# Loads gated on the fifth exponentials, products without use at the start, and a longer load latency in the planner of a Linformer attention and MLP-mixer kernel

## The chip, the cores and the metric

The kernel runs on one core of one Trainium2 chip, in one launch. The metric is the device time of one execution in microseconds (us), as the median of the runs. A separate execution was taken by the hardware profiler; all rows, windows and transfers quoted here come from that one.

## The reference

For 8 batches, 8 heads, 1024 positions and 64 channels in a head, attention with projected keys and values (`E` and `F` are 64 x 1024), then an MLP mixer over positions (256 wide) and over channels (512 to 1536 to 512):

```python
k_proj = einsum('ks,bhsd->bhkd', E, k);  v_proj = einsum('ks,bhsd->bhkd', F, v)
scores = q @ k_proj.T / 8;  attn = softmax(scores)         # over 64 projected keys
x = (attn @ v_proj).transpose(0, 2, 1, 3).reshape(B, S, H * D)
h = relu(x.transpose(0, 2, 1) @ w_tok1) @ w_tok2
u = x + h.transpose(0, 2, 1)
out = u + relu(u @ w_ch1) @ w_ch2
```

Inputs and output are float32; the kernel works in bf16 with float32 sums.

## The kernel before

**Two parts for each batch.** `front(b)` does attention and the token mixer, `channel(b)` the channel mixer. In a front, a projection multiplies k and v with E and F (L423 and L427, side by side in the two halves of TensorE's columns; batch 0 uses L484 and L491). `attend(h)` scores each head (L535), VectorE takes the maxima and subtracts them (L544, L545), ScalarE takes the exponentials (L551), and the weights are transposed, from batch 1 on by a DMA transpose that SP issues (L578, tile `eT`; batch 0 uses TensorE, L586, with a copy, L589). In batch 0, for the heads in `DIRECT`, the subtraction is folded into eight small ScalarE instructions (L564, with L557 and L558 on VectorE). `weigh` multiplies the weights with v for a group of heads (L630) and normalises (L596, L597, L642); the groups are heads 0 to 2, 3 to 5, and 6 and 7 from batch 1 on. `tok1` (L662) and `tok2` (L750; batch 0 L692) are the token mixer; their sum `u` is transposed for the channel mixer (`uT`: by SP from batch 1 on, L769; batch 0 by TensorE, L733). q is transposed by TensorE in batches 0 and 1 (L518) and by SP from batch 2 on (L794). `channel(b)` multiplies up (L860, 96 matmuls of 512 columns in a batch) and down (L903), adds `u` (L914) and stores (L919, SP).

**The order of instructions is planned.** Each step is an operation with an engine (or a choice of two), an estimated time, dependences, buffers and a rank. `Planner.plan` walks through estimated time: of the operations that are ready it takes the one that could start first, the front's before the channel's where both could, and writes it at the end of its engine's queue. On the chip each engine keeps to that order and waits by semaphores where the estimate was too short. Loads are issued by POOL, and the planner keeps one clock for all transfers:

```python
dma = max(t + w + 1.8, dma) + o.dma                      # a load from POOL, w = 0.72
dma = max(t + 1.0, dma) + o.dma                          # a transfer from SP; end = dma + 1.0 + DMA_SLACK
```

`o.dma` is the transfer's size by an assumed rate (`READ`, `WRITE`, `TURN`), and `DMA_SLACK` is 1.5 us.

**When loads are issued.** All of batch 0, the first weights and batch 1 are issued from the start, in the order of `LOADS`: a small letter with a number is a pair of heads of batch 0, a capital one a half of batch 1, `wt1`, `wt2` and `wc1a`, `wc1b` are weights. Everything later waits behind a gate: `later(at, *seen)` looks `at` up in `GATES`, and where there is an entry, POOL copies one element of a tile (L331, `mark`), so that it waits until that tile is written, and then issues the loads of the entry (L290; the halves of `w_ch2`, `w0` and `w1`, L337). The key `(b, h)` waits for the `eT` of head h of batch b, `(b, "t")` for the last `uT` of batch b - 1 and the last q transpose of batch b, `(b, "u")` for the last `uT` of batch b. Batches share five input buffers (`ins_pool`), each of which holds the k, the v or the q of one batch.

`RK` holds the ranks of batch 0's projections, weighings and token mixing.

Of the kernel before, what the change touches and what calls it, by code (L numbers as in the profile page):

```python
# [16 lines left out]

LOADS = ("k0", "q0", "q1", "k1", "k3", "v1", "q3", "k2", "q2", "v0", "wt1", "v3", "wt2", "v2",  # L20
         "V0", "wc1a", "K0", "Q0", "Q1", "V1", "K1", "wc1b")
GROUPS0 = ((0, 1), (2, 3), (4, 5), (6, 7))
DIRECT = (5, 7)
ADDED = (0, 1, 2, 3)
SUMMED = (0, 1, 2, 3)
RK = (-37, -7, 82)


GATES = {(0, "u"): ("w0",), (1, 0): ("w1",), (1, 4): ("k2", "v2", "q2"), (1, "u"): ("k3",), (2, "t"): ("v3",),
         (2, 7): ("q3",), (3, "t"): ("k4", "v4"), (3, 7): ("q4",), (4, "t"): ("k5", "v5"),  # L30
         (4, 7): ("q5",), (5, "t"): ("k6", "v6"), (5, 7): ("q6",), (6, "t"): ("k7", "v7"), (6, 7): ("q7",)}


AFTER = {"PE": 0.2, "DVE": 0.15, "ACT": 0.15}
# [4 lines left out]
def dve(n, kind="f32"):  # L39
    return 0.08 + (0.00104 * n + 0.075 if kind == "f32" else 0.00052 * n + 0.07)  # L40
# [35 lines left out]
class Planner:  # L76
# [6 lines left out]
    def op(self, eng, fn, deps=(), new=(), bufs=(), prio=0, dma=0.0, behind=()):  # L83

        o = Op()
        o.eng, o.fn, o.deps, o.new = eng, fn, [d for d in deps if d], list(new)
        o.prio, o.dma = prio, dma
        o.bufs = list(dict.fromkeys(list(new) + list(bufs)))
        for b in o.bufs:
            b.left += 1  # L90
        o.seq, o.waiting, o.after, o.ready = len(self.ops), 0, [], 0.0
        o.behind, o.next = list(behind), []
        self.ops.append(o)
        return o

    def plan(self, start):
        for o in self.ops:
            o.waiting = len(o.deps) + len(o.behind)
            for d in o.behind:
                d.next.append(o)  # L100
            for d in o.deps:
                d.after.append(o)
        free = dict(start)
        dma = 3.4
        ready = [o for o in self.ops if not o.waiting]
        order = []
        while ready:
            best = None
            for o in ready:
                at = o.ready  # L110
                ok = all(b.slot is not None or b in o.new for b in o.bufs)
                for b in o.new:
                    slot = b.pool.best()
                    ok = ok and slot is not None
                    at = max(at, slot[0]) if slot else at
                if not ok:
                    continue
                for e, w in o.eng.items():
                    key = (max(at, free[e]), o.prio, w, o.seq)
                    if best is None or key < best[0]:  # L120
                        best = (key, o, e)
            assert best is not None, "no operation can go on"
            (t, _, w, _), o, e = best
            ready.remove(o)
            for b in o.new:
                f, i = b.pool.best()
                b.pool.free_at[i] = None
                b.slot = i
            if e == "POOL":
                free[e] = t + w  # L130
                if o.dma:
                    dma = max(t + w + 1.8, dma) + o.dma
                    end = dma + (DMA_SLACK if o.prio[0] > 0 else 0.0)
                else:
                    end = t + w + 0.3
            elif e == "PE":
                free[e] = t + w
                end = t + w + AFTER[e] + (SLACK if o.prio[0] > 0 else 0.0)
            elif e == "SP":
                free[e] = t + w  # L140
                dma = max(t + 1.0, dma) + o.dma
                end = dma + (1.0 if o.prio[0] >= 0 else 0.6) + (DMA_SLACK if o.prio[0] % 2 == 0 else 0.0)
            else:
                free[e] = t + w - 0.08
                end = t + w + AFTER[e] - 0.08 + (SLACK if o.prio[0] > 0 else 0.0)
            for b in o.bufs:
                b.left -= 1
                b.until = max(b.until, end)
                if not b.left:
                    b.pool.free_at[b.slot] = b.until  # L150
            for a in o.after + o.next:
                a.waiting -= 1
                a.ready = max(a.ready, end if a in o.after else t)
                if not a.waiting:
                    ready.append(a)
            order.append((t, end, e, o))
        assert len(order) == len(self.ops)
        return order
# [3 lines left out]
def kernel(  # L162
# [13 lines left out]
    nc = tc.nc  # L176
    P = 128

    B, H, S, D = q.shape
# [26 lines left out]
    bank_any = Pool_(banks)  # L206
# [17 lines left out]
    ident = sb.tile([P, P], BF16, name="ident")  # L224
# [20 lines left out]
    op = pl.op  # L245

    def f32(buf, *shape):
        t = buf.t
        n = 1
        for s_ in shape:  # L250
            n *= s_
        t = t[:, :n]
        if len(shape) == 2:
            return t.rearrange("p (a b) -> p a b", b=shape[1])
        return t
# [19 lines left out]
    def load(fn, prio, nbytes, deps=(), new=(), bufs=()):  # L275
        behind = [latest[0]] if latest else []
        latest[:] = [op({"POOL": 0.72}, lambda e: fn(), deps, new, bufs, prio, nbytes / READ, behind)]
        return latest[0]
# [35 lines left out]
    ld = {}  # L314
    for name in LOADS:
        if name in weights:
# [8 lines left out]
    def later(at, *seen):  # L325

        what = GATES.get(at)
        if not what:
            return
        b = at[0]  # L330
        gate = [op({"POOL": 0.1}, lambda e, of=of: nc.gpsimd.tensor_copy(out=mark, in_=of()), [dep], [],  # L331
                   [buf], prio=(2 * b, 0, len(pl.ops))) for buf, of, dep in seen]
        for w in what:
            if w[0] == "w":
                cs = slice(int(w[1]) * CC // 2, (int(w[1]) + 1) * CC // 2)
                ld_wc2[int(w[1])] = load(
                    lambda cs=cs: nc.gpsimd.dma_start(  # L337
                        out=wc2_sb[:, cs, :], in_=moe_w_ch2.rearrange("(cc p) d -> p cc d", p=P)[:, cs, :]),
                    (0, len(pl.ops)), DM * DC * 2, gate)
            else:  # L340
                load_in(int(w[1]), w[0], 0, H, (2 * b, 0, len(pl.ops)), gate)

    mk_ident = op({"POOL": 0.55}, lambda e: make_identity(nc, ident), prio=(0, 0.5))


    stage = Buf(gT_pool)
# [6 lines left out]
    for i, w in enumerate((E, F)):  # L353
# [3 lines left out]
        for g in range(2):  # L357
# [14 lines left out]
            def ef_c(e, i=i, sl=sl, pb=pb):  # L372
                if i == 0:
                    copier(e)(out=EFT_sb[:, sl, :KP], in_=b16(pb, NSI, KP)[:, sl])
                else:
# [4 lines left out]
            o = op({"ACT": 1.15, "DVE": 0.7}, ef_b, [ld_ef], [], [stage], (0, -90 + i, g))  # L380
            o = op({"PE": 0.5}, ef_t, [o, mk_ident], [pb] if g == 0 else [], [pb, stage],
                   prio=(0, -90 + i, g))
# [6 lines left out]
    def last_u(b):  # L389
        return uTs[b], lambda: uTs[b].t[0:1, NSI - 1, 0, 0:1], uT_at[b][NSI - 1][-1]  # L390
# [4 lines left out]
    def front(b):  # L395
# [8 lines left out]
        def pr():  # L404
            n_[0] += 1
            return (lvl, rank[0], n_[0])
# [6 lines left out]
        qTb = Buf(qT_pool)  # L413
# [97 lines left out]
        def attend(h):  # L511
# [56 lines left out]

            if first and h in DIRECT:
                om = op({"DVE": dve(512) + 0.2}, rmax, [os_], [], [sc, mx], pr())  # L570
# [221 lines left out]
        if b >= TURN_Q:  # L792
            for h0 in range(0, H, 4):
                o = op({"SP": 3.5}, lambda e, h0=h0: nc.sync.dma_start_transpose(  # L794
                    out=qTb.t[:, h0 : h0 + 4].rearrange("p h t c -> p (h t) c"),
                    in_=qin.t[:, h0 : h0 + 4].rearrange("p h s d -> p (h s d)")),
                    [landed[b, "q", h0]], [qTb] if h0 == 0 else [], [qin, qTb], pr(),
                    dma=4 * S * D * 2 / TURN)
                for h in range(h0, h0 + 4):
                    qt_at[h] = o  # L800
            later((b, "t"), last_u(b - 1), (qTb, lambda: qTb.t[0:1, H - 1, 0, 0:1], o))
        for h0, h1 in chunks:
            rank[0] = RK[0] + 2 * h0 if first else 0
            (project_first if first else project)(h0, h1)
            for h in range(h0, h1):
# [5 lines left out]
                if h in group_of_last:  # L811
                    rank[0] = 2 * h + RK[1] if first else 0
                    if first and group_of_last[h] in SUMMED:
# [3 lines left out]
                    if first:  # L817
                        heads = groups[group_of_last[h]]
                        rank[0] = 2 * h + RK[2]
                        for i in range(TC):  # L820
# [14 lines left out]
    def channel(b):  # L835
# [92 lines left out]
        for si in range(NSI):  # L928
            if (b, si) == (B - 1, NSI - 1):
                down_by_columns(si, (DM // 2, DM // 4, DM // 4))  # L930
            else:
                down(si)

    front(0)
    for b in range(B):
        if b + 1 < B:
            front(b + 1)
        channel(b)
# [35 lines left out]
```

## Time and profile before

| | |
|---|---|
| median of 3 runs (lowest, highest) | 471.61 us (470.45, 471.82) |
| the profiled execution's own time | 473.21 us |
| its span | 471.3 us |
| TensorE busy | 454.7 us (96%) |
| VectorE, ScalarE busy | 271.2 us (58%), 177.6 us (38%) |
| mean granted TensorE clock | 0.993 |
| read from HBM, written to it | 59.24 MB, 16.78 MB |

The span runs from the first instruction to the last; 1.9 us of the profiled execution's time lie around it. A row of the timeline gives the start, the length, the engine, the line, the operation with what it writes and reads, and how many instructions are merged; in brackets stands the idle time of the engine before it and what ended that. Where a row merges several matmuls, its end holds the last one's way through the array, so a matmul's cost is taken from the distance of starts: 0.216 us for 512 columns at the full clock.

### The profile page before, as it was taken

To read this page: it belongs to the slowest core of one execution; us is meant where nothing else is said; L and a number is where in the kernel's file an instruction comes from. 1 tells how busy PE (TensorE), PEld (TensorE's weight loads), DVE (VectorE), ACT (ScalarE), POOL (GpSimd) and SP (SyncE) were. 2 spreads that over 40 slices of the span, in tenths; PEclk is the share of its full clock that TensorE was granted. 3 is DMA by queue.
4 is the path that set the end of the run, shared out by engine and by line. 5 is a ranking of instruction groups with operands and counts; after the bars stand their busy time and mean duration, and the time that the engine had idled before them with its cause. 6 is when DMAs were issued, how large, how long until landed. Compare 5 with 4: busy or idle time off the path is not lost.

```text
span 471.3 us, 7555 instructions
## 1 busy us (share of the span) xinstructions
PE 454.7 (96%) x2916; PEld 238.4 (51%) x2916; DVE 271.2 (58%) x624; ACT 177.6 (38%) x333; POOL 37.3 (8%) x67
## 2 busy tenths in 40 slices
PE   4799996999999999999999999999999999999996
PEld 3696553445545445545554455545545455544444
DVE  5987673349475579439655478528665388521022
ACT  4867630117510472207610374116520375105600
POOL 7420020010000100010000100010000000000000
PEclk9999998899999999999999999999999999999999
DMA  9999999889689896879489995889489221351022
GB/s 168 208 207 208 166 152 236 149 165 171 98 175 179 171 171 113 185 143 226 70 164 184 197 160 77 175 176 226 74 163 194 90 56 35 57 167 45 1 89 91
DMA packets 122885, 68.14 MB, mean 145 GB/s; under 512 B 86752, under 2 KB 114272, under 8 KB 122848
## 3 DMA queue, kind: packets, MB, share of 16 engines
q0 software_dynamic: 28192, 29.36, 39.9%
q1 hardware_dynamic: 94656, 38.29, 38.2%
q8 instruction: 23, 0.38, 0.3%
q14 instruction: 14, 0.11, 0.1%
HBM read 59.24 MB, written 16.78 MB: 161 GB/s over the span
## 4 chain that ended last, share of the span: by engine, by line
PE 89%; DMA 6%; ACT 2%; POOL 1%; DVE 1%; issue 0%; POOLq 0%
PE bank L860 34%; PE bank L903 33%; PE bank L662 6%; PE bank L750 5%; DMA in<-in_v_dram 3%; PE bank L535 3%; PE bank L630 3%; PE bank L423 2%; DMA in<-in_q_dram 1%; DMA eT<-ex 1%; PE bank L692 1%; PE bank L427 1%; ACT ex L551 1%; PE bank L518 1%; PE bank L733 0%
## 5 line engine op out<-in xcount | busy, mean ns | idle before, releaser
L860 PE MATMUL bank<-uT,wc_sb 128*128 128x512 bf16 x768 | 178.6, 379 | 0.0
L903 PE MATMUL bank<-wc_sb,gT 128*128 128x512 bf16 x756 | 171.4, 379 | 0.0
L265 ACT ACTIVATE gT<-bank 128x512 bf16<-128x512 f32 x169 | 100.5, 595 | 96.9 <-PE bank L860 95.4
L903 PEld LDWEIGHTS <-gT 128*128 128x128 bf16 x756 | 72.5, 98 | 82.8 <-issue 1.6
L860 PEld LDWEIGHTS <-wc_sb 128*128 128x128 bf16 x768 | 71.7, 98 | 73.8 <-issue 0.2
L914 DVE TENSOR_TENSOR o<-bank,u 128x512 f32<-128x512 f32 x63 | 43.3, 690 | 109.4 <-PE bank L903 109.3
L544 DVE TENSOR_REDUCE mx<-bank 128x8 f32<-128x512 f32 x62 | 42.3, 682 | 30.1 <-PE bank L535 30.1
L642 DVE TENSOR_TENSOR x<-bank,rd 128x384 bf16<-128x384 f32 (+1 forms) x100 | 48.7, 498 | 3.5 <-ACT ex L564 0.5
L545 DVE TENSOR_TENSOR sh<-bank,mx 128x512 f32<-128x512 f32 x62 | 42.9, 692 | 4.6
L759 DVE TENSOR_TENSOR u<-bank,x 128x512 bf16<-128x512 f32 x56 | 34.2, 683 | 18.0 <-PE bank L750 18.0
L551 ACT ACTIVATE ex<-sh 128x512 bf16<-128x512 f32 x62 | 39.0, 629 | 9.2 <-DVE sh L545 7.3
L437 ACT CAST kp<-bank 64x512 bf16<-64x512 f32 (+1 forms) x8 | 4.2, 525 | 85.1 <-PE bank L427 84.9
L662 PE MATMUL bank<-x,wt_sb 128*128 128x512 bf16 (+1 forms) x176 | 30.4, 328 | 0.0
L630 PEld LDWEIGHTS <-eT 128*128 128x128 bf16 x256 | 19.0, 97 | 13.3 <-issue 1.2
L750 PE MATMUL bank<-hT,wt_sb 128*128 128x512 bf16 x112 | 25.3, 379 | 0.0
L630 PE MATMUL bank<-vbd,eT 128*128 128x130 bf16 x256 | 23.9, 220 | 1.1 <-DVE sh L545 0.7
L535 PEld LDWEIGHTS <-qT 128*128 128x128 bf16 x256 | 18.3, 100 | 9.7 <-ACT qT L528 0.2
L265 ACT ACTIVATE hT<-bank 128x512 bf16<-128x512 f32 (+1 forms) x20 | 9.2, 473 | 35.8 <-PE bank L662 35.6
L535 PE MATMUL bank<-kbd,qT 128*128 128x128 bf16 x256 | 22.3, 222 | 0.2 <-ACT qT L528 0.2
L662 PEld LDWEIGHTS <-wt_sb 128*128 128x128 bf16 x176 | 14.7, 99 | 14.8 <-issue 2.6
L750 PEld LDWEIGHTS <-wt_sb 128*128 128x128 bf16 x112 | 16.1, 144 | 8.4
L427 PE MATMUL bank<-in,EFT_sb 128*64 128x512 bf16 (+1 forms) x64 | 15.3, 386 | 3.8 <-DMA in<-in_v_dram 3.8
(72 smaller groups left out, 228.0 us busy)
## 6 DMA issues: line engine op xcount, KB each, us to landing
out_dram<-o SPq DMA_DIRECT2D x63, 256.0 KB, 2.6
in<-in_k_dram POOLq DMA_DIRECT2D x6, 1024.0 KB, 10.3
in<-in_v_dram POOLq DMA_DIRECT2D x6, 1024.0 KB, 16.8
in<-in_q_dram POOLq DMA_DIRECT2D x6, 1024.0 KB, 9.8
wc_sb<-in_moe_w_ch_dram POOLq DMA_DIRECT2D x4, 768.0 KB, 20.7
in<-in_k_dram POOLq DMA_DIRECT2D x4, 256.0 KB, 7.3
in<-in_q_dram POOLq DMA_DIRECT2D x4, 256.0 KB, 7.6
in<-in_v_dram POOLq DMA_DIRECT2D x4, 256.0 KB, 11.1
```

What stands on the lines that cost most here:

```text
L265: nc.scalar.activation(out=out, in_=in_, func=ACT.Relu)
L535: nc.tensor.matmul(f32(sc, NT, 2 * KP)[:, t, :], qT.t[:, h, t, :], bd.t[0][:, h // 2, h % 2, :], start=True, stop=True,)
L544: nc.vector.reduce_max(out=mx.t, in_=s_, axis=AX.X)
L545: nc.vector.tensor_tensor(out=sh.t, in0=s_, in1=mx.t[:, :, None].to_broadcast([P, NSI, KP]), op=ALU.subtract,)
L551: nc.scalar.activation(out=ex.t, in_=sh.t.rearrange("p (t s) k -> p t (s k)", s=2), func=ACT.Exp, scale=scale,)
L630: nc.tensor.matmul(ou[:, i], eTs[h].t[:, t, :], bd.t[1][:, h, :], start=True, stop=True)
L642: nc.vector.tensor_tensor(out=xb.t[:, t, heads[0] : heads[0] + n], in0=ou[:, :, :, 0:D], in1=r.to_broadcast([P, n, 2, D]), op=ALU.mult,)
L662: nc.tensor.matmul(f32(pb, n), wt1_sb[:, si, i * P : (i + 1) * P], xrow(si, a, z), start=(si == 0), stop=(si == NSI - 1),)
L750: nc.tensor.matmul(f32(pb, DM), wt2_sb[:, i, si::NSI], hb.t[:, i, :], start=(i == 0), stop=(i == TC - 1),)
L860: nc.tensor.matmul(f32(pb, 4, P), wc1_sb[:, dc, cc * P : (cc + 1) * P], uT.t[:, sj * 4 : (sj + 1) * 4, dc, :], start=(dc == 0), stop=(dc = ...
L903: nc.tensor.matmul(f32(pb, DM), g.t[:, cc, (si % 4) * P : (si % 4 + 1) * P], wc2_sb[:, cc, :], start=(cc == 0), stop=(cc == CC - 1),)
L914: nc.vector.tensor_tensor(out=ob.t, in0=f32(pb, DM), in1=u.t[:, si, :], op=ALU.add)
```

## The change

- `LOADS` has another order: q1 ahead of q0, q3 ahead of k3, `wt2` ahead of v3, and K0 ahead of V0, K1 ahead of V1, Q1 last, with `wc1a` ahead of them all.
- `DIRECT` holds heads 2, 3, 4, 5 and 7 of batch 0 instead of 5 and 7.
- `FILL` adds 40 matmuls of the identity with itself at the start, of the lowest rank, whose result nobody reads.
- `RK` has other values.
- `GATES`: in batches 1 to 6 the k, v and q of the next batch are issued together when the `eT` of head 4, the fifth, has landed. For batch 1 this is so before. For the others, before, k and v waited for `(b, "t")` (k3 for `(1, "u")`), and q for the `eT` of head 7. The call with `(b, "t")` is gone.
- The planner takes a load's latency as 3.8 us instead of 1.8.

Line numbers in the text are those of the kernel before.

```diff
--- before.py
+++ after.py
@@ -17,18 +17,18 @@
 
 
 
-LOADS = ("k0", "q0", "q1", "k1", "k3", "v1", "q3", "k2", "q2", "v0", "wt1", "v3", "wt2", "v2",
-         "V0", "wc1a", "K0", "Q0", "Q1", "V1", "K1", "wc1b")
+LOADS = ("k0", "q1", "q0", "k1", "q3", "k3", "v1", "k2", "q2", "v0", "wt1", "wt2", "v3", "v2",
+         "wc1a", "K0", "V0", "Q0", "K1", "V1", "Q1", "wc1b")
 GROUPS0 = ((0, 1), (2, 3), (4, 5), (6, 7))
-DIRECT = (5, 7)
+DIRECT = (2, 3, 4, 5, 7)
 ADDED = (0, 1, 2, 3)
 SUMMED = (0, 1, 2, 3)
-RK = (-37, -7, 82)
-
-
-GATES = {(0, "u"): ("w0",), (1, 0): ("w1",), (1, 4): ("k2", "v2", "q2"), (1, "u"): ("k3",), (2, "t"): ("v3",),
-         (2, 7): ("q3",), (3, "t"): ("k4", "v4"), (3, 7): ("q4",), (4, "t"): ("k5", "v5"),
-         (4, 7): ("q5",), (5, "t"): ("k6", "v6"), (5, 7): ("q6",), (6, "t"): ("k7", "v7"), (6, 7): ("q7",)}
+FILL = 40
+RK = (-16, -9, 96)
+
+
+GATES = {(0, "u"): ("w0",), (1, 0): ("w1",),
+         **{(b, 4): (f"k{b + 1}", f"v{b + 1}", f"q{b + 1}") for b in range(1, 7)}}
 
 
 AFTER = {"PE": 0.2, "DVE": 0.15, "ACT": 0.15}
@@ -129,7 +129,7 @@
             if e == "POOL":
                 free[e] = t + w
                 if o.dma:
-                    dma = max(t + w + 1.8, dma) + o.dma
+                    dma = max(t + w + 3.8, dma) + o.dma
                     end = dma + (DMA_SLACK if o.prio[0] > 0 else 0.0)
                 else:
                     end = t + w + 0.3
@@ -343,6 +343,13 @@
     mk_ident = op({"POOL": 0.55}, lambda e: make_identity(nc, ident), prio=(0, 0.5))
 
 
+    idle = Buf(bank_any)
+    for i in range(FILL):
+        op({"PE": 0.09}, lambda e: nc.tensor.matmul(
+            f32(idle, P), ident, ident, start=True, stop=True), [mk_ident],
+            [idle] if i == 0 else [], [idle], (99, i))
+
+
     stage = Buf(gT_pool)
     eft = {}
 
@@ -798,7 +805,6 @@
                     dma=4 * S * D * 2 / TURN)
                 for h in range(h0, h0 + 4):
                     qt_at[h] = o
-            later((b, "t"), last_u(b - 1), (qTb, lambda: qTb.t[0:1, H - 1, 0, 0:1], o))
         for h0, h1 in chunks:
             rank[0] = RK[0] + 2 * h0 if first else 0
             (project_first if first else project)(h0, h1)
```

## The prediction

> **What bounds the kernel now.** I read first the busy rows and slices of the page, then TensorE's waits and timeline, then the loads.
>
> ```profile
> PE 454.7 (96%) x2916; PEld 238.4 (51%) x2916; DVE 271.2 (58%) x624; ACT 177.6 (38%) x333; POOL 37.3 (8%) x67
> PE   4799996999999999999999999999999999999996
> PEclk9999998899999999999999999999999999999999
> ```
>
> TensorE is the bound: full in all slices but the first three, the seventh and the last. So only two places can give time, the first 25 us and the neighbourhood of 80 us; a new wait of TensorE anywhere else adds its whole length. The seventh and eighth slices also show the granted clock dip. Here is TensorE's timeline there (start, us, what):
>
> ```profile
> 76.34 0.40 PE L423 MATMUL bank<-in,EFT_sb 128*64 128x512 bf16 x1
> 80.53 0.59 PE L427 MATMUL bank<-in,EFT_sb 128*64 128x512 bf16 x1 [3.79 <-DMA in<-in_v_dram]
> ...
> 84.04 4.67 PE L662 MATMUL bank<-x,wt_sb 128*128 128x512 bf16 x16
> 88.54 1.89 PE L903 MATMUL bank<-wc_sb,gT 128*128 128x512 bf16 x8
> ```
>
> And the windows around it (TensorE's busy time is the third number, the granted clock stands behind the engines):
>
> ```profile
> 80.00:84.00 4.00, 3.47 (x15) 1.48 (x14) 0.00 (x0) 0.00 (x0) 0.00 (x0) 0.50 1.18 252
> 84.00:90.00 6.00, 6.00 (x24) 2.50 (x24) 0.69 (x1) 2.35 (x4) 0.00 (x0) 0.82 0.60 109
> ```
>
> The projection of batch 2 waits 3.79 us for its v, and then the clock is at 0.50. From 76.34 to 88.54, 12.2 us, TensorE did a projection and `tok1`. At the full clock these take 8 pairs at 0.216 (1.7 us) and 3.56 (the chain's L662 row of the next batch): 5.3 us. The wait therefore cost 6.9 us, 3.8 idle and 3.1 of slow work.
>
> **The gates, batch 1 to 2: a gain of 6.7 us.** Gate (1,4) is the same in both. What differs is TensorE's order: I summed the changed program's matmuls in their order at 0.2158 (512 columns), 0.058 (130) and 0.056 (128) us. Between the first projection of batch 1 and that of batch 2 lie 42.05 us of work instead of 38.6, since `tok1` (16 matmuls, 3.45) now stands ahead. TensorE comes to the projection at 76.34 + 3.45 = 79.8 instead of 76.3; v landed at 80.5. It also scores head 4 some 2.4 us earlier, so the gate opens no later. A rest of 0 to 0.7 us stays, too short to resemble the one idle time after which the clock fell; I take 0.2. Gain 6.9 - 0.2 = 6.7.
>
> **The gates, batches 2 to 6: a loss.** Before, k and v were issued ahead of the scores and q behind the eighth transpose. All eT transposes but the last ones ran beside loads, and the order gave them room: L630 of heads 0 to 2 stood 19 us behind the first scores. Now `later((b,"t"))` and its marks are gone, three loads (6 MB read) start when head 4's transpose lands, and L630 of heads 6 and 7 stands 18.7 us behind the first scores. The last batch of before has the same order of scores and L630 to 0.1 us, without loads, so I lay the new load on its rows:
>
> ```profile
> 382.65 0.39 PE L535 MATMUL bank<-kbd,qT 128*128 128x128 bf16 x4
> 385.51 0.62 ACT L551 ACTIVATE ex<-sh 128x512 bf16<-128x512 f32 x1
> 386.36 1.22 SPq L578 DMA_TRANSPOSE eT<-ex  x1
> 389.94 0.62 ACT L551 ACTIVATE ex<-sh 128x512 bf16<-128x512 f32 x1
> 396.15 0.39 PE L630 MATMUL bank<-vbd,eT 128*128 128x130 bf16 x4
> ```
>
> Head 4 is scored at 382.65, its transpose issued at 386.36 and landed 2.4 to 2.5 later, 388.8. From a landing to the issue behind the gate POOL took 0.64 (62.56 to 63.20), so k goes at 389.45. (The planner's account gives that transpose 1.0 + 0.85 + 1.0 + 1.5 = 4.35 us, so the order was made for loads that go 1.9 later.) Head 7's exponentials end at 390.56: its transpose is issued at 390.6 at the earliest (391.35 in this trace), **1.1 to 1.9 us behind k**. TensorE needs it at 396.15. What does an SP transfer take that goes so soon behind a load? Issues of SP in five short windows (count, size, us to landing):
>
> ```profile
> eT<-ex SPq DMA_TRANSPOSE x8, 2.4
> out_dram<-o SPq DMA_DIRECT2D x3, 256.0 KB, 2.4
> out_dram<-o SPq DMA_DIRECT2D x1, 256.0 KB, 8.4
> out_dram<-o SPq DMA_DIRECT2D x2, 256.0 KB, 8.9
> eT<-ex SPq DMA_TRANSPOSE x1, 6.4
> ```
>
> The first two are without loads (380 to 392, 256 to 261). Then a store 1.1 behind k (207.5, k at 206.40), two stores 1.3 and 2.2 behind k (155.36), and the transpose of 56.18, 2.1 behind the second half of `wc2` (54.08). So head 7's transpose lands 2.4 us after its issue if nothing hinders it (before it is needed: wait 0), and 10.5, the longest that a transpose took beside loads, if it fares worst (401.1, wait 5). I take the row nearest in distance, 8.4: 390.6 + 8.4 = 399.0, a wait of 2.8. Batches 2 and 5 have this spacing; in 3 and 6 head 7 is scored 0.9 later, most of which DVE, still behind, evens out; in batch 4 L630 stands 0.9 later (wait 1.9). Sum 4 x 2.8 + 1.9 = **13.1 us**, between 0 and 24. Nothing covers it: channel work that could is behind L630 in TensorE's order, and SP's stores behind head 7 wait as well.
>
> What else moves with the gates is covered: v lands at most 18.4 us after k's issue, and the next projection stands 27 behind it; q (21.6 after its own issue in the group of three at 63.2) lands 11 us or more before the next scores; the uT transposes, first needed 12 us after their issue, take 10.5 at worst. Without that cover each would add what it is late.
>
> **The start: nothing.** V0 is third of the three transfers that end with it, where K0 was; the bytes ahead are the same, and that place landed at 17.96 + 18.48 = 36.44. The projection of batch 1 began at 36.54 and stands in the same place of the order (22.8 us of useful work ahead). So a faster start gains 0.1 at most. Under this cover lie:
> - `FILL`: 26 products stand ahead of E's transposes, 12 behind, 2 ahead of the first q. Two q transposes (x8) took 1.03 us at 8.54 and 0.61 at 15.58, so one is 0.13 us early and 0.06 later. From the identity at 2.64, 26 end at 6.0 at the latest, and E's transposes began at 5.15: up to 0.9 late. This reaches the first scores only through q0, which lands 1.3 us later than it did; uncovered, 40 products cost 2.2 to 5.2.
> - `LOADS`: q0 and q1 change places, a delay of up to 1.3 us, about what the clock gives back.
> - `DIRECT`: heads 2, 3 and 4 save L545 (0.69) less L558 (0.17) on DVE, 1.6 us in all, and cost ACT 1.74 - 0.63 each, 3.3 us. DVE was busy 9.7 of the 10 us from 15 to 25, ACT 8.8.
> - `RK` and the planner's 3.8 only reorder.
>
> Together -0.1 to +1.5; taken 0.
>
> **Sum.** Profiled: span 471.3 (473.21 with what lies around it). -6.7 + 13.1 = +6.4: span 477.7. The profiled execution is 1.6 above the median of the runs, so for the median 471.6 + 6.4 = **478.0**.
>
> **Rivals.**
> 1. *The eighth transpose is not held up: faster.* Speaking for it: transposes and load packets do run side by side, and a lone transpose has 544 packets (the queue's count in a window of one). At 1:1 with loads at 150 packets per us (the trace's packets between 113 and 118 us) it needs 1.0 + 3.6 us, landing at 395.2, ahead of 396.15. Against: every SP transfer behind a load above took 6.4 or more. No waits: 471.6 - 6.7 = 464.9. It decides below a latency of 5.5 us; at 6.9 gain and loss balance. The Trainium skill's "DMA: Bandwidth & Descriptors" (Queues, rings and completion order) says that each DMA engine alternates between its queues packet by packet; by that rule this rival holds, while the 8.4 and 8.9 above disagree.
> 2. *The waits also cost the clock.* Each would lose up to 2.8 more, as at 80 us (5.65 us at half speed behind the wait): all five, 478 + 14 = 492; one or two, 481 to 484. For: the clock fell there 2.6 us after the idle time began. Against: 2.8 is shorter than 3.79. The Trainium skill's "TensorE: Matmul & The Clock Gate" (Part 1) has the clock fall after an idle window of about 3.4 us; the one fall here, after 3.79, agrees, and by that rule this rival would not come about.
> 3. *Balance.* A latency near 6.9 makes waits of 1.3: 471.6, no change.
>
> That the wait at 80 us stays as it is, so that the change misses its aim, has no room: the 3.45 us of `tok1` are in the order.
>
> **Numbers.** Forecast 0.48 (474 to 482), rival 1 0.33, rival 2 0.12, rival 3 0.07. Slower takes the forecast and rival 2: 0.60; faster 0.33; same 0.07, within 0.3%, about what a measurement of this kernel can tell. Since both signs are likely, the range runs from just under rival 1's time, 464, to 486, with one to three clock falls; beside it stands the forecast's own 474 to 482.
>
> **What would show it.** Right: no wait at L423/L427 and no clock dip near 80 us; project of batch 1 still at 36 to 37.5; in batches 2 to 6 the first L630 of heads 6 and 7 waiting 2 to 4 us for `eT`, whose last transposes land 7 us or more after issue. Wrong: those landing within 5 us, or a first projection of batch 1 after 38.

## The result and the profile after

The changed kernel takes **498.44 us** (median of six) against 471.03 us for the kernel before (468.79 to 472.71): a ratio of 1.0577, 95% interval 1.0526 to 1.0627. The ratio goes by the five runs of 495.44 to 500.42 us; the sixth, at 503.40, was in the slow state and is left out of it. The forecast was 478.0 us, with a range of 464 to 486: the direction was right, the size was not. The profiled execution took 497.21 us with a span of 495.4, that is 24.0 us more than the profiled one of before (473.21, span 471.3).

After the change most lines of the front stand 7 further down: L630 is now L637, L423 and L427 are L430 and L434; L860 and L903 are L866 and L909. The page's busy row and slices:

```profile
PE 462.0 (93%) x2928; PEld 242.0 (49%) x2956; DVE 266.6 (54%) x622; ACT 183.6 (37%) x356; POOL 35.9 (7%) x56
PE   6799999996999989995999996999869999999996
PEclk9999999998999999998899998999979999999999
```

The dip in the seventh slice is gone, and so is the one of the clock there. In its place stand four deep dips of TensorE (slices 10, 19, 25 and 30), with the clock below full in the same slices. TensorE's waits (line waited for: us in total, times, longest):

```profile
PE bank L637 <- DMA eT<-ex: 21.1, 6, 5.9
PE bank L348 <- POOL ident masks.py:199: 2.7, 1, 2.7
```

L637 is the weighing. Its waits for `eT` add up to 21.1 us: 4.18, 1.38, 5.92, 4.30 and 0.32 + 4.96 us in batches 2 to 6. The wait of the projection for v has left the list. The timeline at both places (start, us, what; idle time before it in brackets):

```profile
77.89 1.03 PE L909 MATMUL bank<-wc_sb,gT 128*128 128x512 bf16 x4
78.85 0.40 PE L430 MATMUL bank<-in,EFT_sb 128*64 128x512 bf16 x1
...
117.06 0.22 PE L637 MATMUL bank<-vbd,eT 128*128 128x130 bf16 x1
121.47 0.51 PE L637 MATMUL bank<-vbd,eT 128*128 128x130 bf16 x3 [4.18 <-DMA eT<-ex]
```

The projection of batch 2 goes at 78.85, with no idle time ahead (`tok1` stands before it, and v landed at 78.57). The weighing of heads 6 and 7 of batch 2 begins with one matmul and then stands still for 4.18 us. The windows there, and behind the longest wait (TensorE's busy time is the third number; clock, DMA share and GB/s end the row):

```profile
118.00:119.00 1.00, 0.00 (x0) 0.00 (x0) 0.00 (x0) 0.00 (x0) 0.00 (x0) 1.00 1.22 196
119.00:120.00 1.00, 0.00 (x0) 0.00 (x0) 0.00 (x0) 0.00 (x0) 0.00 (x0) 0.75 1.21 196
120.00:121.00 1.00, 0.00 (x0) 0.00 (x0) 0.00 (x0) 0.00 (x0) 0.00 (x0) 0.50 1.30 194
121.00:122.00 1.00, 0.53 (x4) 0.45 (x5) 0.17 (x2) 0.00 (x0) 0.00 (x0) 0.50 1.25 209
...
236.00:239.00 3.00, 3.00 (x9) 1.08 (x8) 1.05 (x4) 0.60 (x1) 0.00 (x0) 0.51 1.24 206
```

All engines are idle for 118 to 121 while the DMA engines are full: the loads of batch 3 run, and TensorE waits for a transpose that shares them. The granted clock falls to 0.50 during the wait and stays there behind it. By the clock's records it was at half from 119.49 for 6.83 us, from 232.13 for 6.83, from 303.81 for 3.41 and from 361.84 for 6.83. What of these stretches lies behind the ends of the waits (121.47, 233.07, 303.31, 363.14) is 4.85, 5.89, 3.41 and 5.53 us; half of each is lost: 2.4 + 2.95 + 1.7 + 2.8 = 9.8 us.

So the account of the span is: waits +21.1, slow clock behind them +9.8, the 6.9 us at 80 us gone, and a first projection of batch 1 at 35.94 instead of 36.54, -0.6. Sum +23.4, measured +24.1.

Why did the transposes come late? Issue times from the trace, in us, for heads 6 and 7 and the k load that goes behind head 4's landing:

| batch | k issued | head 6: to k's issue, to landing | head 7: to k's issue, to landing |
|---|---|---|---|
| 2 | 110.38 | -0.27, 6.17 | +1.12, 9.92 |
| 3 | 170.98 | -1.16, 2.92 | +0.14, 6.74 |
| 4 | 220.31 | -0.12, 6.12 | +1.19, 11.52 |
| 5 | 292.07 | -0.23, 4.50 | +1.16, 10.04 |
| 6 | 351.38 | -0.41, 6.94 | +0.97, 10.74 |

Head 7's transpose goes 1.0 to 1.2 us behind k in four batches, as predicted, and takes 9.9 to 11.5 us, not 8.4. Head 6's goes 0.1 to 0.4 ahead of k and is caught as well; it stands before head 7's in SP's queue. The queues' packets in batch 2 show how (packets, MB, share of 16 engines; q0 carries POOL's loads, q1 what SP issues). By the packets' records a transpose is 512 packets with data and, behind them, 32 of four bytes. From 111.2 to 112.1 head 6's data went, in 0.8 us, with no load beside them:

```profile
q1 hardware_dynamic: 512, 0.13, 70.9%
```

From 112.1 to 116.35 the first load's packets went, and of SP's queue only head 6's 32 last ones; head 6's transpose landed at 116.28:

```profile
q0 software_dynamic: 495, 0.51, 101.6%
q1 hardware_dynamic: 32, 0.00, 1.0%
```

From 116.35 to 121.2 head 7's went between the load's:

```profile
q0 software_dynamic: 785, 0.79, 100.2%
q1 hardware_dynamic: 544, 0.13, 23.8%
```

So head 7's transpose, issued at 111.50, lost time twice. Its first packet went only at 116.41, behind the last one of head 6's (115.94), and its data then took 4.5 us instead of 0.8, to land at 121.42. In batches 4 to 6 it is the same: head 7's first packet goes 0.1 to 2.0 us behind head 6's last, and its data take 4.7 to 5.3 us. The Trainium skill's "DMA: Bandwidth & Descriptors" (Queues, rings and completion order) has each DMA engine alternate between the queues; the last stretch agrees roughly, 544 to 785. The one before it, 32 to 495, does not test that, since nothing of head 7's went ahead of head 6's last packets. What held these back until 1.3 to 3.9 us behind the data is not shown.

### The profile page after: what moved, and what is told of

It reads as the page before. It is cut to its first block, busy times and chain, and to the rows that moved or that the text cites. A ratio compares the mean times of both kernels' runs of the same rounds, so it can differ in the third digit from the quotient of the medians.

```text
span 495.4 us, 7578 instructions
## 1 busy us (share of the span) xinstructions
PE 462.0 (93%) x2928; PEld 242.0 (49%) x2956; DVE 266.6 (54%) x622; ACT 183.6 (37%) x356; POOL 35.9 (7%) x56
## 4 chain that ended last, share of the span: by engine, by line
PE 84%; DMA 12%; DVE 2%; POOL 1%; issue 1%; ACT 0%; POOLq 0%; DVEq 0%
PE bank L909 33%; PE bank L866 30%; DMA eT<-ex 10%; PE bank L669 6%; PE bank L757 5%; PE bank L430 3%; PE bank L542 3%; PE bank L637 2%; DMA in<-in_v_dram 2%; POOL in L290 1%; PE bank L699 1%; PE bank L740 0%; PE bank L888 0%; PE bank L525 0%; PE bank L463 0%
## 5 line engine op out<-in xcount | busy, mean ns | idle before, releaser
L866 PE MATMUL bank<-uT,wc_sb 128*128 128x512 bf16 x768 | 186.2, 388 | 0.0
L909 PE MATMUL bank<-wc_sb,gT 128*128 128x512 bf16 x734 | 170.3, 382 | 1.7 <-issue 0.7
L265 ACT ACTIVATE gT<-bank 128x512 bf16<-128x512 f32 x178 | 105.8, 595 | 123.7 <-PE bank L866 122.8
L909 PEld LDWEIGHTS <-gT 128*128 128x128 bf16 x756 | 74.0, 99 | 89.1 <-issue 5.0
L866 PEld LDWEIGHTS <-wc_sb 128*128 128x128 bf16 x768 | 72.9, 100 | 75.1 <-issue 5.4
L551 DVE TENSOR_REDUCE mx<-bank 128x8 f32<-128x512 f32 x59 | 40.3, 682 | 9.4 <-PE bank L542 9.0
L637 PE MATMUL bank<-vbd,eT 128*128 128x130 bf16 x256 | 24.1, 229 | 22.1 <-DMA eT<-ex 21.1
L552 DVE TENSOR_TENSOR sh<-bank,mx 128x512 f32<-128x512 f32 x59 | 40.8, 692 | 5.1 <-ACT ex L558 0.5
L558 ACT ACTIVATE ex<-sh 128x512 bf16<-128x512 f32 x59 | 37.1, 629 | 8.0 <-DVE sh L552 6.8
L637 PEld LDWEIGHTS <-eT 128*128 128x128 bf16 x256 | 18.9, 102 | 34.0 <-DMA eT<-ex 23.0
L603 DVE TENSOR_SCALAR rd<-bank 128x6 f32<-128x6 f32 (+2 forms) x88 | 13.7, 156 | 24.0 <-PE bank L637 23.6
L331 POOL COPY mark<-eT 1x1 bf16<-1x1 bf16 x7 | 1.2, 177 | 301.1 <-DMA eT<-ex 301.1
L669 PEld LDWEIGHTS <-wt_sb 128*128 128x128 bf16 x176 | 14.8, 98 | 13.3
```

What stands on the lines that cost most here:

```text
L265: nc.scalar.activation(out=out, in_=in_, func=ACT.Relu)
L551: nc.vector.reduce_max(out=mx.t, in_=s_, axis=AX.X)
L552: nc.vector.tensor_tensor(out=sh.t, in0=s_, in1=mx.t[:, :, None].to_broadcast([P, NSI, KP]), op=ALU.subtract,)
L558: nc.scalar.activation(out=ex.t, in_=sh.t.rearrange("p (t s) k -> p t (s k)", s=2), func=ACT.Exp, scale=scale,)
L637: nc.tensor.matmul(ou[:, i], eTs[h].t[:, t, :], bd.t[1][:, h, :], start=True, stop=True)
L669: nc.tensor.matmul(f32(pb, n), wt1_sb[:, si, i * P : (i + 1) * P], xrow(si, a, z), start=(si == 0), stop=(si == NSI - 1),)
```

## The experiments

All times are medians, with the ratio to the kernel before measured beside it and its 95% interval. Rows bear each kernel's own line numbers: the weighing is L640, L629 or L638 in some. Theory A of the texts on record: the load that starts behind head 4 catches the transposes of heads 6 and 7, and the waits cost the clock as well; the rest of the change gains a little. The rivals are in each text.

**Later loads, by a delay.** In the changed kernel, POOL copies one element 16 times, or 8 times, ahead of each k of batches 3 to 7; the plan does not know of it.

```diff
         def go():
+            if b >= 3 and which == "k":
+                for _ in range(16):   # 8
+                    nc.gpsimd.tensor_copy(out=mark, in_=ident[0:1, 0:1])
```

> The changed kernel, but in front of the k load of batches 3 to 7 POOL makes 16 one-element copies (0.18 us each by the L331 rows, some 2.9 us in all) of which the planner knows nothing: the order on TensorE, DVE, ACT and SP stays, the loads of batches 3 to 7 go some 3 us later, behind the issue of head 7's transpose instead of 1.1 us ahead of it. Theory A (the loads overtake the eighth transpose, which costs 21.1 us of waits at L637 and 9.8 us of half clock): the waits go, the clock stays full, 498.4 - 30.9 = 467 us, about 0.99 of the kernel before. Rival B (three loads in one burst are too much for the transfers around them, whoever goes first): the waits stay or move to the projection or the q transposes, 485 us or more.

> The same with 8 copies, some 1.5 us: the k load goes about 0.4 us behind the issue of head 7's transpose. If what decides is whose packets are queued first (the transpose's first packet comes 1.0 us after its issue, a load's 1.4 us after its own), there is no wait: 467 us. If the load only shares the transfer engines with the transpose, packet by packet, from the time both have packets, the transpose loses at most a few tenths of a us here and would have lost about 2 us in the changed kernel, not the 5 to 9 us that it did: also 467 us, but then the changed kernel's latencies stay unexplained. If a load hinders a transpose that is already under way, waits of 2 to 4 us stay: 485 us.

With 16 copies: 465.83 us, 0.9872 [0.9839, 0.9905]. No wait for `eT` is left in TensorE's list, and the transposes of batch 2 land as without loads (window 104 to 124, median us to landing):

```profile
in<-in_k_dram POOLq DMA_DIRECT2D x1, 1024.0 KB, 9.3
...
eT<-ex SPq DMA_TRANSPOSE x6, 2.4
```

Head 7's goes 2.1 to 3.6 us ahead of k here. Some 32.6 us of the changed kernel's time hang on the loads going a few microseconds earlier. With 8 copies: 472.61 us, 0.9994 [0.9960, 1.0028], between the two expectations, since the batches split:

```profile
PE bank L640 <- DMA eT<-ex: 4.5, 2, 2.6
```

| batch | 2 | 3 | 4 | 5 | 6 |
|---|---|---|---|---|---|
| head 7's issue against k's (us) | -0.80 | -1.87 | -0.13 | -0.87 | -0.71 |
| to landing (us) | 2.55 | 2.45 | 7.50 | 2.39 | 7.94 |

A transpose issued 0.8 us or more ahead of k takes 2.4 to 2.6 here; one issued 0.7 ahead, 7.9. So "not behind a load" is not enough. But the distance of the issues is not what decides: in the kernel with 60 products below, head 7's of batch 3 is issued only 0.51 ahead of k and takes 2.44. There its last packet goes at 171.54 and the load's first at 171.56. Here in batch 4 the load's first packet goes at 215.68, while head 7's data are just going through; its four-byte packets come at 217.84 to 220.86, and it lands at 221.19. So the latency goes by whether the transpose's last packets are through when the load's first one goes, 1.7 to 2.1 us behind the load's issue in the changed kernel. In batches 2 to 6 of all kernels here whose k waits for head 4 or 7, head 7's took 2.4 to 4.1 us where they were and 6.7 to 12.3 where they were not. Where only head 7's is caught (here in batches 4 and 6, in the changed kernel in batch 3) it takes 6.7 to 7.9; where head 6's is caught ahead of it, 9.9 to 11.5 in the changed kernel.

**Later loads, by the gate.** The gates of batches 2 to 6 at the eighth head instead of the fifth; everything else as changed, so that the planner knows of it.

```diff
-         **{(b, 4): (f"k{b + 1}", f"v{b + 1}", f"q{b + 1}") for b in range(1, 7)}}
+         (1, 4): ("k2", "v2", "q2"), **{(b, 7): (f"k{b + 1}", f"v{b + 1}", f"q{b + 1}") for b in range(2, 7)}}
```

> The changed kernel with the gates of batches 2 to 6 at the eighth transpose instead of the fifth (batch 1's stays at the fifth), the planner knowing it. Theory A: no wait at L637; k goes 4.9 us later, v lands 18.4 us behind k at most, about 35 us after the first scores, and the projection stands 38 us after them: no wait there. 467 us. Rival B: three loads still go in one burst, 485 us or more.

465.49 us, 0.9864 [0.9836, 0.9893]: faster than both kernels, and the best version here, level with the 16 copies. Head 7's transpose goes 3.0 to 3.8 us ahead of k in every batch and takes 2.4. From the third slice on TensorE is full:

```profile
PE   6799999999999999999999999999999999999996
PEclk9999999999999999999999999999999999999999
```

The loads go 3.9 to 4.6 us later against head 7's transpose than head 4's gate let them (3.0 to 3.8 behind it instead of 0.1 to 1.2 ahead), and nobody misses them, since the next projection stands far behind. So grouping the three loads and dropping the `(b, "t")` gates costs nothing; the place of the gate does.

**The old gates in the changed kernel.** `GATES` and the call of `later((b, "t"), ...)` as before.

> The changed kernel with the gates of before: what is left of the change is the order of the first loads, DIRECT, FILL, RK and the planner's 3.8. Theory A: the gain at 80 us (6.9 us) without the loss: 464 to 465 us, 0.985 to 0.99 of the kernel before. Rival B says the same of the loss. Rival C (the rest of the change costs something too, at the start or by another order): 468 us or more.

470.29 us, 0.9985 [0.9959, 1.0010], not the expected 464 to 465. No wait for `eT` is left, but another wait has come, the rival of that text (timeline of this kernel):

```profile
102.42 1.03 PE L868 MATMUL bank<-uT,wc_sb 128*128 128x512 bf16 x4
105.67 0.61 PE L543 MATMUL bank<-kbd,qT 128*128 128x128 bf16 x4 [2.23 <-DMA qT<-in]
```

The scores of batch 2 wait for the last transposes of q: with the old gate, k of batch 3 was issued at 91.79. The q transpose issued 2.9 us ahead of it took 4.3 us, and the one issued 0.7 us behind it 13.1: it landed at 105.62, and the scores began at 105.67. It is the same collision with another victim: wherever a load starts beside SP's transposes, whoever needs these next may wait. This wait of 2.23 us, too, brought the clock to half, from 105.56 for 3.41 us.

**The new gates alone in the kernel before**, without the planner's 3.8 and the edits at the start.

> The kernel before with the new gates alone (no b, t gate; the planner's latency stays 1.8, the start as before). The order puts L630 of heads 6 and 7 18.7 us behind the first scores, as in the changed kernel. Theory A: the wait of 80 us stays (6.9 us) and the waits of batches 2 to 6 come on top with their clock, about 31 us: 500 to 504 us. Rival (the longer latency or the start makes part of the loss): 490 us or less.

501.57 us, 1.0645 [1.0591, 1.0699]. Its two large waits of TensorE that came from loads:

```profile
PE bank L629 <- DMA eT<-ex: 20.6, 5, 5.7
...
PE bank L426 <- DMA in<-in_v_dram: 4.7, 1, 4.7
```

The gates alone make the whole loss. And the wait for v at 80 us is still there: the gates did not take it away.

**k alone behind head 4.** In the changed kernel v and q follow behind head 7.

```diff
+         (1, 4): ("k2", "v2", "q2"), **{(b, 4): (f"k{b + 1}",) for b in range(2, 7)},
+         **{(b, 7): (f"v{b + 1}", f"q{b + 1}") for b in range(2, 7)}}
```

> The changed kernel, but in batches 2 to 6 only k is issued behind head 4's transpose; v and q follow behind head 7's. Theory A: what holds heads 6 and 7 up is the load that starts beside them, and one is enough, since in the changed kernel k's packets alone filled the engines until both transposes had landed (heads 7's land within 0.5 us of k). Then waits of 4 to 6 us in batches 2, 4, 5 and 6, the clock falls as in the changed kernel, and 490 to 499 us. Rival: it is the three loads queued together that hold the transposes up; then k alone takes about half of the waits, fewer clock falls, 474 to 485 us.

494.28 us, 1.0492 [1.0452, 1.0532]:

```profile
PE bank L638 <- DMA eT<-ex: 18.8, 7, 4.4
```

One load is enough: head 7's transposes still take 9.6 to 10.6 us in batches 2, 4, 5 and 6. v and q add 2.3 us of waits.

**The waits filled with work.** In the changed kernel 60 products of the identity, whose result nobody reads, stand ahead of the first L637 of heads 6 and 7 in batches 2, 4, 5 and 6. They keep TensorE busy where it waited, so the clock should stay.

> The changed kernel with 60 products of the identity that nobody reads (3.4 us at the full clock) ahead of the first L637 of heads 6 and 7 in batches 2, 4, 5 and 6, whose waits were 4.2 to 5.9 us. They fill idle time, so that 0.8 to 2.6 us of each wait is left, and the transposes land no sooner. Theory A, with the clock as its second term: the clock falls no more or once, the 9.8 us of half clock go: 488 to 490 us. If the falls were not made by these waits, or cost no time, 498 us; if the products only come on top, 510 us.

489.09 us, 1.0383 [1.0344, 1.0421]: some 9 us less than the changed kernel, with 240 matmuls more. Busy row and wait of this kernel:

```profile
PE 468.1 (96%) x3168; PEld 253.5 (52%) x3196; DVE 266.2 (55%) x622; ACT 183.6 (38%) x356; POOL 35.4 (7%) x56
...
PE bank L640 <- DMA eT<-ex: 8.2, 4, 4.2
```

The products take 240 x 0.056 = 13.4 us; with the 8.2 that remain this is 21.6, about the 21.1 of waits in the changed kernel. (Not batch by batch: the 1.38 of batch 3 is gone, and batch 6's transpose took 12.3 us, so that 4.2 remain there.) The idle time was in sum only filled, and yet the span fell by 8.1 us (495.4 to 487.3). That is the clock: one fall is left, behind the wait of 4.19 us in batch 6, for 3.41 us at half speed (1.7 lost), and 9.8 - 1.7 = 8.1.

**What gains: the planner's latency, and the start.** Three kernels: the kernel before with the latency of 3.8 alone; the kernel before with 3.8 and the gates of the best version; and the best version with `FILL = 0`.

> The kernel before with the planner's load latency 3.8 and nothing else. In the order tok1 of batch 1 now stands ahead of the projection of batch 2. If that alone ends the wait at the projection (3.8 us and the clock behind it), 465 to 468 us; the later gates then cost nothing, as in the kernel before. Rival: the longer latency also moves q's or other loads' users, and a new wait appears elsewhere (as 2.2 us for the q transposes in the kernel with the old gates), 469 to 472 us.

> The kernel before with the planner's 3.8 and the gates of batches 2 to 6 at the eighth transpose (batch 1's at the fifth), the start (LOADS, DIRECT, FILL, RK) as before. If the latency is what moves tok1 ahead of the projection of batch 2 and takes the 6.9 us, and the start gives nothing: 464 to 466 us. If the start's edits give 1 us or more: 466 to 468.

> The kernel with the gates at the eighth transpose (465.5 us), without the 40 products of the start. If the start is set by the landing of the first half of batch 1 (its projection began 0.1 us behind that landing), as in the prediction, no difference beyond 1 us: 465 to 466. If the products' warm clock is what lets TensorE be ready by then, the projection comes later by what the colder clock costs, up to 1.5 us: 467.

| kernel | median us | ratio to before, 95% interval |
|---|---|---|
| before, latency 3.8 | 469.02 | 0.9966 [0.9936, 0.9995] |
| before, latency 3.8, gates of the best | 468.16 | 0.9944 [0.9918, 0.9971] |
| best without `FILL` | 467.44 | 0.9931 [0.9912, 0.9951] |
| best | 465.49 | 0.9864 [0.9836, 0.9893] |

The latency alone puts `tok1` ahead of the projection of batch 2 (timeline of the kernel before with 3.8):

```profile
76.45 4.54 PE L662 MATMUL bank<-x,wt_sb 128*128 128x512 bf16 x16 [1.06 <-DVE x L642]
80.92 0.40 PE L423 MATMUL bank<-in,EFT_sb 128*64 128x512 bf16 x1
```

The wait for v is gone and a wait of 1.06 us for VectorE has come, with the clock full throughout. Against the profiled execution of before this is 473.21 to 468.04, 5.2 us; between the medians it is only 1.7 (470.72 to 469.02). So the gain of the latency alone is hardly clear of the noise (the interval ends at 0.9995). The kernel before spreads more from run to run (468.1 to 473.7 beside these) with a mean granted clock of 0.992 to 1.0; the profiled execution, at 0.993, is one of those that lost most.

The orders of `LOADS`, `DIRECT` and `RK` show no gain clear of the noise (468.16 to 467.44). `FILL` is worth 0.7% (the two intervals do not overlap), 2 to 3 us; the two kernels were not run beside each other, only each beside the kernel before. The same step of the start, first in the best version without it:

```profile
6.78 1.06 PE L491 MATMUL bank<-EFT_sb,in 128*64 128x64 bf16 x32 [0.80 <-DMA in<-in_k_dram]
9.66 1.89 PE L525 MATMUL bank<-ident,in 128*128 128x128 bf16 x16 [1.28 <-DMA in<-in_q_dram]
```

and then in the best version itself:

```profile
6.94 0.70 PE L491 MATMUL bank<-EFT_sb,in 128*64 128x64 bf16 x32 [0.20 <-DMA in<-in_k_dram]
9.39 1.07 PE L525 MATMUL bank<-ident,in 128*128 128x128 bf16 x16 [0.67 <-DMA in<-in_q_dram]
```

The 32 small products of the first k take 0.70 instead of 1.06 us and the 16 transposes of q 1.07 instead of 1.89: by the clock's records TensorE is at the full clock from 5.45 us on instead of 13.57. The first projection of batch 1 goes at 35.80 instead of 36.66, though its V0 landed at the same time, 35.37 and 35.36. That is 0.9 of the 1.8 us between the two spans (463.7 and 465.5). A wait of 0.5 us for `eT` at 71.41 stands in the kernel without `FILL` alone; where the rest arises was not followed.

## Why the prediction was right in direction and wrong in size

**The gain at 80 us: the term held, its cause was misplaced.** Without wait or clock dip at L430, `tok1` ahead, 6.9 us gone from the profiled execution, where 6.7 were taken. But the prediction booked it under the gates and said that "`RK` and the planner's 3.8 only reorder". The reorder was the gain: the gates alone kept the wait (4.7 us), the 3.8 alone ended it. Set against the median it was too large: the profiled execution had 2 us more to lose than the typical one, and taking its whole loss off the median takes off more than the typical execution has to lose.

**The loss at the weighings: the spacing held, the term of 13.1 was mis-sized.** "1.1 to 1.9 us behind k" came as 0.1 to 1.2. The failed step is "I take the row nearest in distance, 8.4", together with the "4 x 2.8 + 1.9" that follows from it: the row is of a single store with nothing of its queue in front. Here head 6's transpose was caught as well, issued 0.1 to 0.4 ahead of k, and head 7's stood behind it. Where head 6's is free, the row is about right: in the kernel before with the new gates, batch 4, head 6's took 2.6 us, and head 7's, 0.5 behind k, 8.5. The prediction laid head 6 aside without a word, as if a transfer issued ahead of a load were safe; with eight copies a transpose issued 0.7 us ahead was caught. The 9.9 to 11.5 us measured were near the longest case (10.5) that the text named, and 21.1 lies inside its 0 to 24. By batch the forecast was off too: batch 4, taken as the shortest wait (1.9), had the longest (5.92).

**The clock: the step that failed most.** Rival 2 was right in its mechanism and had a chance of 0.12; it came true together with the forecast, and its price, up to 2.8 for each wait, was about right too: 1.7 to 2.95, 9.8 us for four. It was set low because "2.8 is shorter than 3.79", so the mis-sized wait undid this step as well. But the reason itself does not hold: waits of 2.23 (old gates) and 2.65 us (eight copies) also brought the clock down. The prediction's own row spoke against it: the clock fell 2.6 us after the idle time began, sooner than the 2.8 us wait that it forecast. Two errors of 8.0 and 9.8 us, both in the same direction, make up most of the 20.4 between 478.0 and 498.44; another 2.8 come from the profiled executions, 1.6 above the median before and 1.2 below it after. The range added one to three clock falls to waits of 13.1 us; it carried neither its own upper bound of 24 for these nor four falls, and so could not hold the time.

**Rival 1, "the eighth transpose is not held up", is refuted for this spacing** (9.9 to 11.5 us to landing) and is what the best version brings about: with 3 us of distance the transposes take 2.4, and the time is 465.5 where the rival had 464.9.

**The start: "nothing" was nearly right in the trace (-0.6, outside its -0.1 to +1.5) and wrong as a whole:** V0 landed at 35.83 instead of the 36.44 taken as a lid, and in the best version the products are worth 2 us or more. The prediction counted them only as something that could delay. By the clock's records it is full from 6.9 us on instead of 14.5; the text had this only as "about what the clock gives back", set against a delay of q0.

## What to carry to other kernels

Before a load is moved, list what the other queue issues from 1 us ahead of its issue until it has landed, the transfer in front of the last one too: each may be held up, and the one that is needed soonest sets the price. (In the kernel before, a transpose of batch 2 issued 9.7 us behind k, with v's load still running and other transposes in front of it, took 7.6 us.) Moving the gate by three heads, some 4 us, turned a loss of 6% into a gain of 1.4%. A wait of 2 us or more on the bounding engine should be priced with the clock behind it, and a gain read from one profiled execution should be set against that execution, not against the median.

## What the runs showed of the hardware

- **A load holds up SP's transposes, even one whose data are through.** In batches 2 to 6, head 7's transpose issued 0.8 us or more ahead of k took 2.4 to 4.1 us, mostly 2.4 to 2.6; from 0.7 ahead on it took 6.7 to 12.3, but for the one at 0.51 ahead whose last packet still went before the load's first (2.44). Head 6's of batch 2 had sent its data by 112.05, ahead of the load's first packet at 112.18, and landed only at 116.28, 0.3 us behind the last of its four-byte packets. The Trainium skill's "DMA: Bandwidth & Descriptors" (Queues, rings and completion order) says that a completion is written only after all earlier writes of that DMA engine, of other queues too; that would fit, and no run here isolates it.
- **In a load's first microseconds SP's queue once moved nothing.** In the kernel before with the new gates, batch 4, head 7's transpose was issued at 233.37, and head 6's had sent its last packet at 234.30. From 234.5 to 236.85 the loads moved 116 packets and SP's queue none; from 236.85 to 241.65 it was 721 to 544. Whether head 7's packets stood ready in the first stretch is not seen.
- **The clock is decided on a fixed grid.** All its changes in the changed kernel lie multiples of 3.413 us apart (119.49 to 232.13 is 33 of them). In the changed kernel and the one before it fell at the end of windows in which TensorE had been idle for 64% to 100%, not at 41% to 46%; over all the traces here it fell at 62% and more and at none of 53% and less. So 2.2 us of idle time are enough where they lie within one window. A wait of 2.23 us (old gates) cost the clock, one of 1.90 that lay across two windows (eight copies) did not. The Trainium skill's "TensorE: Matmul & The Clock Gate" (Part 1) gives the free-running window of about 3.4 us, which agrees. Its rule that the clock falls after an idle window holds here for windows that are not idle throughout.
